# Seven products instead of plain units for the keys of the first 1024 tokens in the third layer

## The chip, the cores and the metric

The kernel runs on one core of one Trainium2 chip. The metric is the device time of one launch in microseconds (us). Before the change, three runs took 1438.44, 1438.20 and 1438.22 us, median 1438.22. The profiled execution, from which every row below comes, took 1439.99 us.

A core has engines that run side by side, each with its own instruction queue which it works off strictly in order: TensorE (PE; PEld are its weight loads), VectorE (DVE), ScalarE (ACT), GpSimd (POOL), and SyncE (SP), which here only issues DMAs. Semaphores make an instruction wait for one on another engine or for a DMA; everything behind it on its own engine then waits as well.

## The reference, cut to what matters

```
def _A_ref(x, wqkv, wo):                 # x: 2048 tokens x 1024, 32 heads of 32
    q, k, v = heads of (x @ wqkv)
    phi = lambda t: jnp.where(t > 0, t + 1, jnp.exp(t)) + 1e-6
    pq, pk = phi(q), phi(k)
    kv = einsum("bhsd,bhse->bhde", pk, v)
    z = sum of pk over the tokens
    ...
x = x + _A_ref(_layernorm(x), A_wqkv, A_wo)
x = x + _B_ref(_layernorm(x), B_W_gate, B_W_up, B_W_down)
x = x + _A_ref(_layernorm(x), A_wqkv, A_wo)      # the third layer, l = 2 in the code
x = x + _B_ref(_layernorm(x), B_W_gate, B_W_up, B_W_down)
```

`_B_ref` is a feed-forward block (1024 to 3584 and back). Everything comes in bf16. What counts below is one thing: in the third layer the queries and keys are products of normalised rows and the columns of `wqkv`, and `phi` is applied to every element of both.

## The kernel before

**Tiles.** The 2048 tokens are four quarters of 512, each of QT = 4 row tiles of 128 tokens. The normalised rows of a quarter are turned by transposing DMAs (L423) into `xnT` tiles, which are the stationary operand of the matmuls. Column halves of 512 of a weight matrix (`k0`, `k1`, `q0`, `q1`) are the moving operand. A plain unit is one row tile times one column half: eight matmuls of 128x512 into one PSUM bank (`project`, L506), followed by `phi`: a relu on ACT out of PSUM (L448), an exponential on ACT (L449), and a join on DVE (L452). For keys, POOL then adds the rows up (`k_sum`, L525 for the first, L527 for the others).

**Seven products.** `blocks(p, first)` computes the same for two quarters at once with a scheme of Strassen's kind: the input is cut into halves of tokens (the two quarters) and of the inner dimension, the weight into halves of the inner dimension and of columns, and seven products replace eight. Each product is four matmuls (`mm`, L690). It needs four sums of the inputs (`sums_x`, L1272 to L1275, on DVE, 16 instructions for two quarters) and four sums of the weight, which an earlier layer left in DRAM and which two DMAs of 1 MB bring in (`tq0`, `tq1` for the queries, `tk0`, `tk1` for the keys; L472). For row tile j the seven products go through four accumulators, qx, qy, qv, qz, in four steps: `one` does mm1 into qx, copies it to qy (L681 on DVE or L683 on ACT), does mm5 into qv and copies that to `qm`; `two` does mm2 into qx (which is then finished and gets its `phi`), mm6 into qy and qz = qy + qm on DVE (L712); `three` does mm7 into qy, qm = qy + qm on DVE (L716) with its `phi`, and mm3 into qz with its `phi`; `four` does mm4 into qy with its `phi`. So mm2 waits for the copy of qx, mm7 for the sum qz, and mm4 for the sum qm.

**The third layer before.** First the keys of quarter 0 by plain units (eight of them), then the queries of quarters 0 and 1 by seven products, with the plain units of the keys of quarter 1 between the steps, two to each j; then the queries of quarter 2 by plain units, then the keys of quarters 2 and 3 by seven products.

**What sets the order.** The emitting Python code calls the steps and units one after another, and each call is followed by a tick. Side work is due at a number of ticks (`later.at`): layer normalisation of the rows of quarters 2 and 3 (statistics, then the scaling of one row tile on DVE, `ln_scale` L183, at the ticks of the table LN_AT, which isn't changed), sums, sends of x to DRAM (`away`, L283), and early sums of quarter 3 for a later stage (the functions `n1`, `n2`, `n3`, `k1`, all of them `op`, L559, four instructions for each row tile, by `make_early`).

**Where tiles lie.** `slot` takes all large tiles of 8 KB per partition, the weights included, from one pool of 16. A tile that gets the place of an older one may be written only when the last reader of the older one is done; which place it gets follows from the order of requests. The scaled rows of quarter 3 are four L183 into one such tile, here called slab2_2. In the kernel before it has the place of the last weight tile of the layer before, which is read for the last time before the third layer begins.

**Weights.** The `ring` loads weights by SP in the order of a plan (`plan_A`), each as soon as its place is free (L40, L472).

Of the kernel before, what the change touches and what calls it, by code (L numbers as in the profile page):

```python
# [14 lines left out]
P = 128  # L15
# [77 lines left out]
class _Net:  # L93
# [372 lines left out]
    def plan_A(self, l):  # L466
        D = self.D
        cols = {"k0": D, "k1": D + NW, "v0": 2 * D, "v1": 2 * D + NW, "q0": 0, "q1": NW}
        for n in ("k0", "k1", "v0", "q0", "q1", "v1", "o0", "o1") if l == 0 else (
                "k0", "k1", "q0", "q1", "tq0", "tq1", "tk0", "tk1", "v0", "v1", "o0", "o1"):  # L470
            if n[0] == "t":
                self.ring.add((l, n), lambda t, n=n: self.nc.sync.dma_start(  # L472
                    out=t[:, :, :].bitcast(F16), in_=self.tw[n[1:]]))
# [6 lines left out]
    def layer_A(self, l, last_ln):  # L480
# [14 lines left out]
        turns = count()  # L495
        by_row = lambda a: a.rearrange("p (i b d) -> p i b d", i=R, d=HD)

        def project(name, l_q, j, between=None):
            w = ring.get((l, name))

            spare = l_q < self.NQ - 1 and next(turns) % 3 == 2 and not (l and l_q < 2)
# [19 lines left out]
        def k_sum(t, cols):  # L521

            pk = self.pk_home(l, t)[:, cols]
            if t == 0:
                nc.gpsimd.tensor_copy(out=ksum[:, cols], in_=pk)  # L525
            else:
                nc.gpsimd.tensor_tensor(out=ksum[:, cols], in0=ksum[:, cols], in1=pk, op=ALU.add)  # L527
# [128 lines left out]
        def blocks(p, first):  # L656
# [4 lines left out]
            r0, r1, t0, t1 = (ring.get((l, n)) for n in (f"{p}0", f"{p}1", f"t{p}0", f"t{p}1"))  # L661
# [23 lines left out]
            def steps(j):  # L685
# [7 lines left out]

                def one():
                    S["X"] = self.ps.tile([P, NW], F32, tag="a", name=f"qx{j}")
                    mm(1, S["X"], True)
                    if p == "k" and j == 2:
# [3 lines left out]
                    copy(S["Y"], S["X"], p == "k" and j)  # L701
                    v = self.kvp.tile([P, NW], F32, tag=f"kv{j % 2 if p == 'q' or j < 2 else 0}", name=f"qv{j}")
                    mm(5, v, True)
                    S["V"] = self.temp(name="qm5")
                    copy(S["V"], v, p == "k" and j)

                def two():
                    mm(2, S["X"])
                    put(S["X"], 0, j, 0)
# [183 lines left out]
        else:  # L893
            ring.load_to(ring.index((l, "tq1")) + 1)
            for j in range(QT):
                later.at(1 + j, lambda j=j: self.sums_x(l, 0, j))
# [7 lines left out]
        else:  # L904
            first = column_major(k_unit, 0)
# [10 lines left out]
        else:  # L916
            run(first)
            k = iter(row_major(k_unit, 1))
            Q = blocks("q", 0)
            todo = [Q[0][0]]  # L920
            for j in range(QT):
                todo += [next(k), Q[j][1], next(k), Q[j][2]] + ([Q[j + 1][0]] if j + 1 < QT else []) + [Q[j][3]]
            q2 = row_major(q_unit, 2)
            make_early([(16 + 3 * j, QT + j) for j in range(QT)], n1, n2, n3, k1)
            run(todo[:-1] + q2[:1] + todo[-1:])
            later.at(1, lambda: ring.load_to(ring.index((l, "tk1")) + 1))
            self.xs[l, 1] = [self.x[self.NS + i][:, :].bitcast(F16).rearrange("p (a n) -> p a n", n=NW)
                             for i in range(QT)]
            for j in range(QT):
                later.at(4 + j, lambda j=j: self.sums_x(l, 1, j))  # L930
            run(q2[1:])
            K = blocks("k", 2)
# [879 lines left out]
```

## Time and profile before

| what | from the profile before |
|---|---|
| median of three runs | 1438.22 us |
| profiled execution | 1439.99 us, of which 1437.9 us are the span of the instructions |
| PE busy | 1427.1 us (99%) |
| DVE, ACT, POOL busy | 1045.2, 623.3, 309.3 us |
| third layer, keys and queries | 730.4 to 821.6 us: PE busy 90.56 of 91.27 us |
| granted clock of PE | full in all 40 slices |

A line of the table of groups reads: line, engine, operation, out<-in, shape, count | busy us, mean ns. A line of a timeline reads: start, duration, engine, line, operation, count, and in brackets the idle time ahead of it with what ended it. Neighbouring instructions of one kind are merged (x4), and the end of an instruction overlaps the start of the next, so that the price of one among its like is the distance between starts.

### The profile page before, as it was taken

To read this page: it belongs to the slowest core of one execution; us is meant where nothing else is said; L and a number is where in the kernel's file an instruction comes from. 1 tells how busy PE (TensorE), PEld (TensorE's weight loads), DVE (VectorE), ACT (ScalarE), POOL (GpSimd) and SP (SyncE) were. 2 spreads that over 40 slices of the span, in tenths; PEclk is the share of its full clock that TensorE was granted. 3 is DMA by queue.
4 is the path that set the end of the run, shared out by engine and by line. 5 is a ranking of instruction groups with operands and counts; after the bars stand their busy time and mean duration, and the time that the engine had idled before them with its cause. 6 is when DMAs were issued, how large, how long until landed. Compare 5 with 4: busy or idle time off the path is not lost.

```text
span 1437.9 us, 21394 instructions
## 1 busy us (share of the span) xinstructions
PE 1427.1 (99%) x7720; PEld 739.7 (51%) x7748; DVE 1045.2 (73%) x2013; ACT 623.3 (43%) x1143; POOL 309.3 (22%) x220
## 2 busy tenths in 40 slices
PE   9999999999999999999999999999999999999998
PEld 4444444444455444545654444445554565555557
DVE  7978698778685666558778886866766864766895
ACT  7872564333325244332058725733443433444301
POOL 1453860010100011110032477510111011111102
PEclk9999999999999999999999999999999999999999
DMA  9950787898559999966983218998878699975575
GB/s 286 240 162 8 172 209 202 278 335 288 200 192 294 323 367 345 291 216 199 302 277 93 70 22 234 287 274 262 268 225 294 228 304 335 274 229 174 193 260 183
DMA packets 367865, 337.74 MB, mean 235 GB/s; under 512 B 110032, under 2 KB 327760, under 8 KB 366736
## 3 DMA queue, kind: packets, MB, share of 16 engines
q1 hardware_dynamic: 359184, 313.57, 73.1%
q10 hardware_dynamic: 7136, 18.88, 3.4%
q0 software_dynamic: 1440, 3.93, 0.7%
q8 instruction: 60, 0.98, 0.3%
q14 instruction: 45, 0.37, 0.1%
HBM read 246.87 MB, written 64.82 MB: 217 GB/s over the span
## 4 chain that ended last, share of the span: by engine, by line
PE 91%; DVE 3%; DMA 2%; ACT 2%; SPq 1%; issue 1%; ACTq 0%; DVEq 0%
PE ps L506 11%; PE yu L1301 9%; PE yg L1301 9%; PE xg L1301 6%; PE xu L1301 6%; PE dy L1447 6%; PE dx L1447 5%; PE i L1154 5%; PE ps L789 4%; PE zu L1301 3%; PE zg L1301 3%; PE my L588 3%; PE dyT L1489 2%; PE mv L588 2%; PE mx L588 2%; PE dy L1489 2%
## 5 line engine op out<-in xcount | busy, mean ns | idle before, releaser
L1301 PEld LDWEIGHTS <-w 128*128 128x128 f16 (+1 forms) x2768 | 270.4, 98 | 297.2 <-issue 4.6
L506 PE MATMUL ps<-w,xnT 128*128 128x512 bf16 x768 | 169.9, 380 | 0.6 <-ACT xnT L361 0.2
L1381 POOL TENSOR_TENSOR h<-m5u,m5g 128x512 f16<-128x512 f32 x28 | 37.1, 1326 | 425.3 <-DVE m5u L1377 252.5
L506 PEld LDWEIGHTS <-xnT 128*128 128x128 bf16 x768 | 74.4, 98 | 90.3 <-issue 1.8
L1301 PE MATMUL xg<-xnT,w 128*128 128x512 f16 x448 | 115.5, 379 | 0.0
L1301 PE MATMUL xu<-xnT,w 128*128 128x512 f16 x448 | 115.0, 380 | 0.0
L1489 PEld LDWEIGHTS <-h 128*128 128x128 f16 x1008 | 98.6, 98 | 12.9
L1381 POOL TENSOR_TENSOR h<-c22u,c22g 128x512 f16<-128x512 f32 x28 | 36.0, 1285 | 289.8 <-DVE c22u L1377 247.8
L1447 PEld LDWEIGHTS <-h 128*128 128x128 f16 x616 | 60.3, 98 | 71.8 <-issue 0.3
L1301 PE MATMUL yu<-s,w 128*128 128x512 f16 x376 | 96.5, 379 | 0.5 <-DVE zu L1357 0.5
L1301 PE MATMUL yg<-s,w 128*128 128x512 f16 x376 | 96.9, 379 | 0.0
L449 ACT ACTIVATE e<-e,eps 128x512 f32<-128x512 f32 x128 | 91.0, 720 | 3.2
L736 POOL TENSOR_TENSOR kvc<-pq,kvc 128x1024 f32<-128x1024 bf16 x32 | 78.5, 2452 | 53.1 <-DVE den L741 32.8
L789 PE MATMUL ps<-T,pqT 128*128 128x512 bf16 x374 | 83.0, 380 | 0.5
L1328 DVE TENSOR_TENSOR h<-yu,r 128x512 f16<-128x512 f32 x56 | 38.6, 690 | 53.8 <-PE yu L1301 53.8
L1325 ACT ACTIVATE r<-yg 128x512 f32<-128x512 f32 x56 | 33.4, 597 | 101.3 <-PE yg L1301 101.3
L527 POOL TENSOR_TENSOR kvc<-kvc,slab 128x512 f32<-128x512 f32 x46 | 57.2, 1249 | 75.9 <-DVE slab L452 72.7
L1447 PE MATMUL dx<-w,h 128*128 128x512 bf16 x327 | 72.5, 380 | 0.5
L448 ACT ACTIVATE e<-ps 128x512 f32<-128x512 f32 x92 | 54.2, 590 | 28.4 <-PE ps L506 27.9
L1154 PEld LDWEIGHTS <-x 128*128 128x128 f16 x504 | 49.3, 98 | 33.5 <-issue 1.9
L1325 ACT ACTIVATE r<-zg 128x512 f32<-128x512 f32 x56 | 32.9, 587 | 76.7 <-PE zg L1301 76.7
L748 POOL TENSOR_TENSOR pq<-pq,den 128x1024 bf16<-128x1024 bf16 x32 | 61.1, 1909 | 6.8 <-DVE den L743 6.8
(286 smaller groups left out, 2630.6 us busy)
## 6 DMA issues: line engine op xcount, KB each, us to landing
w<-in_B_W_gate_dram SPq DMA_DIRECT2D x56, 512.0 KB, 6.4
w<-in_B_W_up_dram SPq DMA_DIRECT2D x56, 512.0 KB, 6.0
w<-ddT SPq DMA_DIRECT2D x21, 896.0 KB, 6.4
w<-td SPq DMA_DIRECT2D x18, 896.0 KB, 5.0
w<-dd SPq DMA_DIRECT2D x18, 896.0 KB, 5.9
x<-away SPq DMA_DIRECT2D x30, 512.0 KB, 7.5
away<-x SPq DMA_DIRECT2D x24, 512.0 KB, 8.1
w<-in_B_W_down_dram SPq DMA_DIRECT2D x12, 896.0 KB, 6.1
```

Of the source, the lines that this page charges most:

```text
L449: self.last_exp = nc.scalar.activation(out=e, in_=e, func=ACT.Exp, scale=-1.0, bias=self.eps6[:, 0:1])
L506: nc.tensor.matmul(by_row(ps), lhsT=self.xnT[l, l_q][:, kt, j * P:(j + 1) * P], rhs=w[:, kt, :].rearrange("p (b i d) -> p i b d", i=R, d=H ...
L588: nc.tensor.matmul(banks[j], lhsT=A(i)[:, j * P:(j + 1) * P], rhs=B(i), start=start and i == 0, stop=i == NS - 1, skip_group_check=True)
L736: nc.gpsimd.tensor_tensor(out=prod, in0=pq_of[sc, j], in1=zrow, op=ALU.mult)
L748: nc.gpsimd.tensor_tensor(out=heads(pq), in0=heads(pq), in1=den[:, :].unsqueeze(2).to_broadcast([P, D // HD, HD]), op=ALU.mult)
L789: nc.tensor.matmul(ps, lhsT=pqT[sc][:, g, j * P:(j + 1) * P], rhs=T[g // 4][:, g % 4, n2 * NW:(n2 + 1) * NW], start=(g == 0), stop=(g == G ...
L1154: nc.tensor.matmul(b[:, w, :], lhsT=B[p][:, w, k, :], rhs=A[p][:, k, :], start=start and w == 0 and k == 0, stop=k == 1, skip_group_check= ...
L1301: nc.tensor.matmul(ps, lhsT=W[w][m][:, k, :], rhs=A[m][:, k, :], start=start and k == 0, stop=k == 3, skip_group_check=True)
L1325: self.last_relu = nc.scalar.activation(out=out, in_=ps, func=ACT.Relu)
L1381: nc.gpsimd.tensor_tensor(out=h[:, 3, :], in0=V["u"], in1=V["g"], op=ALU.mult)
L1447: nc.tensor.matmul(banks[j], lhsT=A(k)[:, j * P:(j + 1) * P], rhs=w[:, i, :], start=start and k == 0, stop=k == self.U - 1, skip_group_che ...
L1489: nc.tensor.matmul(out, lhsT=A[i // 2][:, i % 2, j * P:(j + 1) * P], rhs=B[m][:, i, :], start=start and i == 0 and j == 0, stop=i == NK - ...
```

## The change

The keys of quarters 0 and 1 of the third layer are computed by `blocks("k", 0)`, in the interleaving that the keys of quarters 2 and 3 had already (row tiles 0 and 1 in turns, then 2 and 3). For that:

- The plan of weights loads `tk0` and `tk1` right behind `k0`, and loads them a second time (`tk0b`, `tk1b`) for the late keys: two more DMAs of 1 MB.
- The sums of quarters 0 and 1 (16 DVE instructions, L1275 to L1278 after the change) move from the first ticks of the layer into the end of the down phase of the layer before.
- Between the steps of the queries there is one plain unit to each j instead of two, and it is one of the queries of quarter 2, so that fewer of these are left for the stretch behind.
- For keys `one` is mm1, copy and then mm2 (`second`), and mm5 with its copy (`fifth`) stands at the head of `two`. The early keys' copies all go to ACT; the late ones keep the split of before.
- The early sums of quarter 3 are due at ticks 8 + 3j of the queries' run instead of 16 + 3j, the sums of quarters 2 and 3 at 1 + j of the last plain units; plain units of this layer use only one of the two kinds of PSUM banks.

The core of the diff:

```diff
--- before.py
+++ after.py
@@ -467,10 +467,10 @@
         D = self.D
         cols = {"k0": D, "k1": D + NW, "v0": 2 * D, "v1": 2 * D + NW, "q0": 0, "q1": NW}
         for n in ("k0", "k1", "v0", "q0", "q1", "v1", "o0", "o1") if l == 0 else (
-                "k0", "k1", "q0", "q1", "tq0", "tq1", "tk0", "tk1", "v0", "v1", "o0", "o1"):
+                "k0", "tk0", "tk1", "k1", "q0", "q1", "tq0", "tq1", "tk0b", "tk1b", "v0", "v1", "o0", "o1"):
             if n[0] == "t":
                 self.ring.add((l, n), lambda t, n=n: self.nc.sync.dma_start(
-                    out=t[:, :, :].bitcast(F16), in_=self.tw[n[1:]]))
+                    out=t[:, :, :].bitcast(F16), in_=self.tw[n[1:3]]))
             elif n[0] == "o":
                 c = NW * int(n[1])
                 self.ring.add((l, n), self.wo_v[:, :, c:c + NW])
@@ -492,13 +492,13 @@
 
 
         R = P // HD
-        turns = count()
+        turns, summed = count(), set()
         by_row = lambda a: a.rearrange("p (i b d) -> p i b d", i=R, d=HD)
 
         def project(name, l_q, j, between=None):
             w = ring.get((l, name))
 
-            spare = l_q < self.NQ - 1 and next(turns) % 3 == 2 and not (l and l_q < 2)
+            spare = not l and l_q < self.NQ - 1 and next(turns) % 3 == 2
             ps = (self.ps3 if spare else self.ps).tile([P, NW], F32, tag="b" if spare else "a")
             for kt in range(KT):
                 if between and kt == KT - 2:
@@ -521,7 +521,8 @@
         def k_sum(t, cols):
 
             pk = self.pk_home(l, t)[:, cols]
-            if t == 0:
+            if cols.start not in summed:
+                summed.add(cols.start)
                 nc.gpsimd.tensor_copy(out=ksum[:, cols], in_=pk)
             else:
                 nc.gpsimd.tensor_tensor(out=ksum[:, cols], in0=ksum[:, cols], in1=pk, op=ALU.add)
@@ -658,7 +659,8 @@
 
             xa, xb = self.xnT[l, first], self.xnT[l, first + 1]
             s1, s2, s3, s4 = self.xs[l, first // 2]
-            r0, r1, t0, t1 = (ring.get((l, n)) for n in (f"{p}0", f"{p}1", f"t{p}0", f"t{p}1"))
+            late = "b" if (p, first) == ("k", 2) else ""
+            r0, r1, t0, t1 = (ring.get((l, n)) for n in (f"{p}0", f"{p}1", f"t{p}0{late}", f"t{p}1{late}"))
             t0, t1 = (t[:, :, :].bitcast(F16) for t in (t0, t1))
             A = {1: xa[:, 0:4], 2: xa[:, 4:8], 3: s4, 4: xb[:, 4:8], 5: s1, 6: s2, 7: s3}
             B = {1: r0[:, 0:4], 2: r0[:, 4:8], 3: r1[:, 4:8], 4: t1[:, 0:4], 5: t0[:, 0:4],
@@ -691,22 +693,28 @@
                                          rhs=B[m][:, k, :].rearrange("p (b i d) -> p i b d", i=R, d=HD),
                                          start=start and k == 0, stop=k == 3, skip_group_check=True)
 
+                def fifth():
+                    v = self.kvp.tile([P, NW], F32, tag=f"kv{0 if late and j > 1 else j % 2}", name=f"qv{j}")
+                    mm(5, v, True)
+                    S["V"] = self.temp(name="qm5")
+                    copy(S["V"], v, late and j)
+
+                def second():
+                    mm(2, S["X"])
+                    put(S["X"], 0, j, 0)
+
                 def one():
                     S["X"] = self.ps.tile([P, NW], F32, tag="a", name=f"qx{j}")
                     mm(1, S["X"], True)
-                    if p == "k" and j == 2:
+                    if late and j == 2:
                         S["Y"] = self.kvp.tile([P, NW], F32, tag="kv1", name=f"qy{j}")
                     else:
                         S["Y"] = self.ps3.tile([P, NW], F32, tag="b", name=f"qy{j}")
-                    copy(S["Y"], S["X"], p == "k" and j)
-                    v = self.kvp.tile([P, NW], F32, tag=f"kv{j % 2 if p == 'q' or j < 2 else 0}", name=f"qv{j}")
-                    mm(5, v, True)
-                    S["V"] = self.temp(name="qm5")
-                    copy(S["V"], v, p == "k" and j)
+                    copy(S["Y"], S["X"], late and j)
+                    (second if p == "k" else fifth)()
 
                 def two():
-                    mm(2, S["X"])
-                    put(S["X"], 0, j, 0)
+                    (fifth if p == "k" else second)()
                     mm(6, S["Y"])
                     S["Z"] = self.ps.tile([P, NW], F32, tag="a", name=f"qz{j}")
                     nc.vector.tensor_tensor(out=S["Z"], in0=S["Y"], in1=S["V"], op=ALU.add)
@@ -892,8 +900,6 @@
             steps = self.head()
         else:
             ring.load_to(ring.index((l, "tq1")) + 1)
-            for j in range(QT):
-                later.at(1 + j, lambda j=j: self.sums_x(l, 0, j))
         for i in range(QT if l == 0 else self.NS, self.ST):
             at, lag = (8 + 3 * (i - QT), 2) if l == 0 else LN_AT[i - self.NS]
             self.ln_at(at, l, i, lag)
@@ -901,8 +907,6 @@
                 later.at(at + 3, lambda i=i: self.send_away(i))
         if l == 0:
             first = self.head_units(lambda *a: k_unit(0, *a), lambda *a: q_unit(0, *a), *steps)
-        else:
-            first = column_major(k_unit, 0)
 
         def quarter0():
             self.phi_lag = 3 if l == 0 else 0
@@ -914,23 +918,22 @@
                                                   mybir.EngineType.Activation}):
                 quarter0()
         else:
-            run(first)
-            k = iter(row_major(k_unit, 1))
+            in_turns = lambda b: [b[j + i][n] for j in (0, 2) for n in range(4) for i in range(2)]
+            run(in_turns(blocks("k", 0)))
             Q = blocks("q", 0)
+            q2 = row_major(q_unit, 2)
             todo = [Q[0][0]]
             for j in range(QT):
-                todo += [next(k), Q[j][1], next(k), Q[j][2]] + ([Q[j + 1][0]] if j + 1 < QT else []) + [Q[j][3]]
-            q2 = row_major(q_unit, 2)
-            make_early([(16 + 3 * j, QT + j) for j in range(QT)], n1, n2, n3, k1)
-            run(todo[:-1] + q2[:1] + todo[-1:])
-            later.at(1, lambda: ring.load_to(ring.index((l, "tk1")) + 1))
+                todo += [Q[j][1], q2[j], Q[j][2]] + ([Q[j + 1][0]] if j + 1 < QT else []) + [Q[j][3]]
+            make_early([(8 + 3 * j, QT + j) for j in range(QT)], n1, n2, n3, k1)
+            run(todo)
+            ring.load_to(ring.index((l, "tk1b")) + 1)
             self.xs[l, 1] = [self.x[self.NS + i][:, :].bitcast(F16).rearrange("p (a n) -> p a n", n=NW)
                              for i in range(QT)]
             for j in range(QT):
-                later.at(4 + j, lambda j=j: self.sums_x(l, 1, j))
-            run(q2[1:])
-            K = blocks("k", 2)
-            run([K[j + i][n] for j in (0, 2) for n in range(4) for i in range(2)])
+                later.at(1 + j, lambda j=j: self.sums_x(l, 1, j))
+            run(q2[QT:])
+            run(in_turns(blocks("k", 2)))
         for q in range(1, self.NQ - 1) if l == 0 else ():
             if (l, q) == (0, 1):
                 for i in range(self.U // 2 - 2):
@@ -1511,7 +1514,7 @@
             entry(1)
             mm(6, S2, y)
             for o, i, b in zip(halves(z), ys, halves(m5)):
-                v.tensor_tensor(out=o, in0=i, in1=b, op=ALU.add)
+                self.last_dz = v.tensor_tensor(out=o, in0=i, in1=b, op=ALU.add)
             later.tick()
             mm(2, a12, x)
             put(0, 0, x, True)
@@ -1747,7 +1750,10 @@
                 self.ln_chunk(l, 1, 20, 3, 3, after)
             elif not final:
                 self.ln_later(l + 1, 0, 24, 3, 4, held)
-                self.ln_later(l + 1, 1, 36, 3, 4, held)
+                self.ln_later(l + 1, 1, 35, 3, 4, held)
+                for j in range(QT):
+                    self.later.at((46, 47, 49, 51)[j], lambda j=j: self.behind(
+                        self.last_on if j < 2 else self.last_dz, lambda j: self.sums_x(l + 1, 0, j), (j,)))
             for n in range(2 if (l, c) in ((1, 1), (3, 0)) else 0):
                 self.later.at(2 + n, lambda t=n + (c == 0) * self.NS: self.bring_back(t))
             self.down(l, c, hT, final)
```

Beside the numbers of lines (L690 becomes L692, L712 becomes L720, L716 L724, L559 L560, L683 L685, L1272 to L1275 become L1275 to L1278), three places of the order matter below.

First DVE around the queries' last row tile, before. qz_7279 and qm_7232 belong to row tile 2, qz_7388 to row tile 3, slab_2_7245 is the tile of quarter 3's scaled rows, and pq are the finished queries.

```order
1011 L183 TENSOR_SCALAR slab_2_7245<-x,mv,rstd 128x1024
1012 L716 TENSOR_TENSOR qm_7232<-qy_7225,qm_7232 128x512
1013 L452 SCALAR_TENSOR_TENSOR x<-ps,e 128x512
1014 L559 TENSOR_TENSOR x<-x,slab_2_7245 128x512
1015 L559 TENSOR_TENSOR x<-x 128x512 x3
1016 L452 SCALAR_TENSOR_TENSOR pq_1_7035<-qm_7232,e 128x512
1017 L452 SCALAR_TENSOR_TENSOR pq_0_7034<-qz_7279,e 128x512
1018 L183 TENSOR_SCALAR slab_2_7245<-x,mv,rstd 128x1024
1019 L452 SCALAR_TENSOR_TENSOR pq_1_7035<-qy_7225,e 128x512
1020 L559 TENSOR_TENSOR x<-x,slab_2_7245 128x512
1021 L559 TENSOR_TENSOR x<-x 128x512 x3
```

The same place after the change. qz_7378 is row tile 2, qz_7459 row tile 3, slab_2_7262 the tile of the scaled rows.

```order
1023 L452 SCALAR_TENSOR_TENSOR pq_0_7176<-qz_7378,e 128x512
1024 L183 TENSOR_SCALAR slab_2_7262<-x,mv,rstd 128x1024 x2
1025 L560 TENSOR_TENSOR x<-x,slab_2_7262 128x512
1026 L560 TENSOR_TENSOR x<-x 128x512 x3
1027 L560 TENSOR_TENSOR x<-x,slab_2_7262 128x512
1028 L560 TENSOR_TENSOR x<-x 128x512 x3
1029 L183 TENSOR_SCALAR slab_2_7262<-x,mv,rstd 128x1024 x2
1030 L560 TENSOR_TENSOR x<-x,slab_2_7262 128x512
1031 L560 TENSOR_TENSOR x<-x 128x512 x3
1032 L452 SCALAR_TENSOR_TENSOR pq_1_7177<-qy_7341,e 128x512
1033 L452 SCALAR_TENSOR_TENSOR pq_0_7176<-qx_7424,e 128x512
1034 L720 TENSOR_TENSOR qz_7459<-qy_7429,qm_7436 128x512
```

What were four L183 apart, with joins and sums of the products between, is now one run: four L183 and twelve L560 stand between the joins of row tile 2 and the sum qz of row tile 3. The tile of the scaled rows has another place too: it takes that of the `xnT` tile of quarter 0, whose last reader is mm2 of row tile 3 of the queries, so the first L183 of this run waits for that product on PE.

Behind that sum, on DVE still, the sum qm of row tile 3 follows after four L560 and nine of the sums of quarters 2 and 3:

```order
1036 L560 TENSOR_TENSOR x<-x 128x512 x3
1037 L1275 TENSOR_TENSOR x<-xnT_3_7465 128x4x128
1038 L1277 TENSOR_TENSOR x<-xnT_2_7025,xnT_3_7465 128x4x128
1039 L1276 TENSOR_TENSOR x<-x,xnT_2_7025 128x4x128
1040 L1275 TENSOR_TENSOR x<-xnT_3_7465 128x4x128
1041 L1278 TENSOR_TENSOR x<-xnT_2_7025,x 128x4x128
1042 L1276 TENSOR_TENSOR x<-x,xnT_2_7025 128x4x128
1043 L1277 TENSOR_TENSOR x<-xnT_2_7025,xnT_3_7465 128x4x128
1044 L1278 TENSOR_TENSOR x<-xnT_2_7025,x 128x4x128
1045 L1275 TENSOR_TENSOR x<-xnT_3_7465 128x4x128
1046 L724 TENSOR_TENSOR qm_7436<-qy_7429,qm_7436 128x512
```

In the kernel before, nothing but one L183 stood between the two (qz_7388, then qm_7338). On PE, the twelve matmuls between mm2 of row tile 3 and its mm7 (mm6 and one plain unit) and the ten between mm7 and mm4 (mm7, mm3 and two of a plain unit) are what runs meanwhile.

Last ACT where the early keys end and the queries begin, after the change. qm_7079, qz_7085 and qy_7045 are row tile 2 of the keys, qm_7098, qz_7104 and qy_7062 row tile 3; qv_7185 and qx_7178 are row tile 0 of the queries.

```order
608 L448 ACTIVATE e<-qm_7079 128x512
609 L448 ACTIVATE e<-qz_7085 128x512
610 L449 ACTIVATE e<-e,eps_137 128x512 x2
611 L448 ACTIVATE e<-qm_7098 128x512
612 L448 ACTIVATE e<-qz_7104 128x512
613 L449 ACTIVATE e<-e,eps_137 128x512 x2
614 L448 ACTIVATE e<-qy_7045 128x512
615 L448 ACTIVATE e<-qy_7062 128x512
616 L449 ACTIVATE e<-e,eps_137 128x512 x2
617 L176 ACTIVATE rstd<-mv,eps_139 128x1
618 L685 ACTIVATE qm_7190<-qv_7185 128x512
```

The copies of the first query products (row 618 and the one of qx_7178 right behind it) stand behind three groups of two relus and two exponentials. Before the change there was no such place: the queries began behind plain units, whose `phi` is one relu and one exponential at a time. Further on, for each j of the queries, the order on ACT stays as it was: relu of qm, relu of qz, two exponentials, copy of the next qx; on PE the stretch between mm7 of one row tile and mm2 of the next was mm7, mm3, mm1, mm4 and a plain unit, and is now the same without the plain unit.

## The prediction

> **What bounds the kernel now.** I read the page's shares first, then the table of stretches for the third layer's keys and queries, then the chain of waits, then the timelines of PE, ACT and DVE.
>
> ```profile
> span 1437.9 us, 21394 instructions
> PE 1427.1 (99%) x7720; PEld 739.7 (51%) x7748; DVE 1045.2 (73%) x2013; ACT 623.3 (43%) x1143; POOL 309.3 (22%) x220
> PEclk9999999999999999999999999999999999999999
> ```
>
> PE has 10.8 us without a matmul in the whole span (1437.9 - 1427.1). So a matmul saved is worth its full time, and a stall of PE made anew costs its full time; both count alike.
>
> ```profile
> 720.00:730.37 10.37, 10.37 (x96) 9.23 (x95) 5.22 (x9) 1.18 (x2) 0.00 (x0) 1.00 1.02 356
> 730.37:821.64 91.27, 90.56 (x419) 40.77 (x417) 77.98 (x141) 72.11 (x133) 32.17 (x27) 1.00 0.42 125
> 744.00:786.00 42.00, 41.82 (x194) 18.89 (x193) 33.65 (x54) 35.43 (x71) 13.00 (x11) 1.00 0.27 58
> ```
>
> The columns are the length, then busy time of PE, PEld, DVE, ACT and POOL, then PE's clock, the DMA share and GB/s. In the layer's stretch (second row) PE is busy 90.56 of 91.27 us, but DVE is busy 77.98 (85%) and ACT 72.11 (79%). Neither has much to give. During the queries (third row) PE idles 0.18 us. The question is thus whether ACT and DVE keep up when PE has less to do and their work stands otherwise.
>
> **The saving.** Keys of 1024 tokens are 16 plain units of 8 matmuls, 128; seven products make 112 of them. Sixteen matmuls go, their weight loads with them.
>
> ```profile
> 730.37 13.81 PE ps L506 x64
> ```
>
> This row of the chain gives 13.81 / 64 = 0.216 us for one. Saved: 16 x 0.216 = 3.45 us. The other work changes little in amount: as many relus, exponentials and joins; four more copies for ACT and as many more pairs of sums qz and qm for DVE.
>
> **ACT between mm7 and the next mm2.** Before, the queries go as follows on PE, then on ACT:
>
> ```profile
> 751.36 1.03 PE L690 MATMUL qy<-w,s 128*128 128x512 f16 x4
> 752.22 1.03 PE L690 MATMUL qz<-w,s 128*128 128x512 bf16 x4
> 753.09 1.03 PE L690 MATMUL qx<-w,xnT 128*128 128x512 bf16 x4
> 753.95 0.60 PE L690 MATMUL qv<-w,s 128*128 128x512 f16 x2
> 754.38 1.03 PE L690 MATMUL qy<-w,xnT 128*128 128x512 f16 x4
> 755.24 1.89 PE L506 MATMUL ps<-w,xnT 128*128 128x512 bf16 x8
> 756.97 1.03 PE L690 MATMUL qx<-w,xnT 128*128 128x512 bf16 x4
> ```
>
> ```profile
> 753.24 0.61 ACT L448 ACTIVATE e<-qm 128x512 f32<-128x512 f32 x1
> 753.76 0.58 ACT L448 ACTIVATE e<-qz 128x512 f32<-128x512 f32 x1
> 754.23 1.32 ACT L449 ACTIVATE e<-e,eps 128x512 f32<-128x512 f32 x2
> 755.46 0.58 ACT L683 ACTIVATE qy<-qx 128x512 f32<-128x512 f32 x1
> 758.93 0.28 ACT L176 ACTIVATE rstd<-mv,eps 128x1 f32<-128x1 f32 x1
> 759.12 0.57 ACT L448 ACTIVATE e<-qx 128x512 f32<-128x512 f32 x1
> ```
>
> mm7 starts at 751.36. The relu of qm starts 1.88 us later, the group of two relus and two exponentials takes 2.22 (753.24 to 755.46), the copy of qx 0.58: it ends 4.68 us after mm7's start, at 756.04. The next mm2, at 756.97, doesn't notice, because a plain unit of 1.73 us lies between. After the change that unit is gone from there. PE has mm7, mm3, mm1, mm4 = 16 matmuls, 3.45 us, and then waits for the copy. For row tile 0 the small L176 stands ahead of the copy too (0.19 between the last two rows): 4.87 - 3.45 = 1.42. For row tile 1 three matmuls of a split mm5 help: 4.68 - 19 x 0.216 = 0.58. Row tile 2: 4.68 - 3.45 = 1.23. Together **3.2 us**. The bound below is nothing, if the groups were to start earlier than in the row; it can't be far from 3.2, since mm7 itself (1.03) and the sum qm on DVE come first.
>
> **The seam between keys and queries.** From mm7 of key row tile 2 on, ACT has three such groups (order above, rows 608 to 616), L176 and the copy of the first qv; mm5 of query row tile 2 needs that bank of PSUM back. ACT: 1.88 + 3 x 2.22 + 0.19 + 0.58 = 9.31. PE has until there 34 matmuls, 7.34. Stall **2.0 us**. Inside the keys the same happens once, more mildly: qy of row tile 2 takes the bank of row tile 0's qy, whose join must be done. ACT: 1.88 + 2 x 2.22 + relus and the first exponential 1.71 (two starts 0.52 and 0.47 apart, and 0.72), the join 0.69, the copy 0.58 = 9.30, against 40 matmuls, 8.63: 0.67. I add 0.24 for mm7 of row tile 2, which waits for qz behind a join. Together **0.9 us**; between nothing and twice that.
>
> **DVE at the queries' last row tile.** This is the largest term. These are DVE's rows at the same place before:
>
> ```profile
> 770.49 1.32 DVE L183 TENSOR_SCALAR slab<-x,mv,rstd 128x1024 bf16<-128x1024 f32 x1
> 772.93 0.41 DVE L559 TENSOR_TENSOR x<-x,slab 128x512 f16<-128x512 bf16 x1
> 773.26 2.05 DVE L559 TENSOR_TENSOR x<-x 128x512 f16<-128x512 bf16 x3
> 775.23 0.68 DVE L452 SCALAR_TENSOR_TENSOR pq<-qm,e 128x512 bf16<-128x512 f32 x1
> 776.57 0.81 DVE L183 TENSOR_SCALAR slab<-x,mv,rstd 128x1024 bf16<-128x1024 f32 x1
> 777.29 0.69 DVE L452 SCALAR_TENSOR_TENSOR pq<-qy,e 128x512 bf16<-128x512 f32 x1
> 777.89 0.42 DVE L559 TENSOR_TENSOR x<-x,slab 128x512 f16<-128x512 bf16 x1
> 778.23 1.09 DVE L559 TENSOR_TENSOR x<-x 128x512 f16<-128x512 bf16 x3
> 779.23 0.69 DVE L452 SCALAR_TENSOR_TENSOR x<-ps,e 128x512 bf16<-128x512 f32 x1
> 779.83 0.69 DVE L452 SCALAR_TENSOR_TENSOR pq<-qx,e 128x512 bf16<-128x512 f32 x1
> 780.43 0.69 DVE L712 TENSOR_TENSOR qz<-qy,qm 128x512 f32<-128x512 f32 x1
> 792.20 0.42 DVE L1272 TENSOR_TENSOR x<-xnT 128x512 f16<-128x512 bf16 x1
> 792.53 0.42 DVE L1274 TENSOR_TENSOR x<-xnT,xnT 128x512 f16<-128x512 bf16 x1
> ```
>
> By distances of starts, an L183 is 0.72, four L559 1.34, a join 0.60, a sum qz or qm about 0.69, one of the L1272 kind 0.33. Before, this work is spread out, and a sum that PE needs is never more than a few instructions away. After the change four L183, twelve L560 and two joins stand ahead of qz of row tile 3, and none of it can start before mm2 of that row tile is done, since the scaled rows take the place of the `xnT` tile that mm2 reads last. From that moment DVE needs 4 x 0.72 + 3 x 1.34 + 2 x 0.60 + 0.69 = 8.8 us, and PE has 12 matmuls, 2.59. mm7 waits **6.2 us**. Then qm: four L560 (1.34), nine sums (3.0) and qm (0.68) make 5.0 us, against ten matmuls, 2.16. mm4 waits **2.9 us**. The last sums wait for transposing DMAs of the new rows; those have the 8.8 us to land.
>
> The bounds: a POOL instruction beside them makes these dearer. L183 took 1.32 at 770.49, and four L559 took 2.30 from 772.93 to 775.23, with this one on POOL:
>
> ```profile
> 773.15 1.21 POOL L527 TENSOR_TENSOR kvc<-kvc,x 128x512 f32<-128x512 f32 x1 [1.89 <-DVE x L452]
> ```
>
> At those prices the two waits would grow by 4 x 0.60 + 4 x 0.96 = 6.2. I take the cheap ends: L527 adds up keys, and no keys are made near this place any more. The cheap ends are also the floor.
>
> **What I cost at nothing.** That plain units use one kind of banks only: four of them are there, and no two plain units follow each other closely among the queries any more. The 16 sums of quarters 0 and 1 go into 720 to 730, where DVE is busy 5.22 of 10.37 us (first of the three rows of stretches); at 0.33 each they need 5.4, so they just fit. If not, the last adds of that phase are late by a few tenths: 0 to 0.3. The weights: `tk0` and `tk1` are issued where one query half and `tq0` were:
>
> ```profile
> 723.54 0.53 SPq L40 DMA_DIRECT2D w<-in_A_wqkv_dram  x1
> 724.18 4.36 SPq L472 DMA_DIRECT2D w<-tq  x2
> ```
>
> ```profile
> w<-in_A_wqkv_dram SPq DMA_DIRECT2D x1, 1024.0 KB, 11.2
> w<-tq SPq DMA_DIRECT2D x1, 1024.0 KB, 13.1
> ```
>
> They took 11.2 and 13.1 us to land, at 734.7 and 737.3. mm5 needs `tk0` at 16 matmuls after 730.3, at 733.7, and mm6 `tk1` at 734.6. With these latencies PE would wait 2.7 us. I take nothing, as the two MB of `k0` and `k1` that were ahead of them in the queues until 723 to 724 aren't there now; 0 to 2.7 goes into the range. The second loads of `tk0` and `tk1` are issued during the waits of the last row tile and have over 10 us until the late keys. The late keys hardly change.
>
> **The sum.** -3.45 + 3.2 + 2.0 + 0.9 + 6.2 + 2.9, less the 0.18 that the queries wait already (their third row of stretches), is +11.6 us. On the profiled execution that is 1439.99 + 11.6 = 1451.6. The median of the runs lies 1.77 below the profiled one: 1438.22 + 11.6 = **1449.8 us**.
>
> **The rivals.** What a measurement of this kernel tells from no change is 0.2%, 2.9 us: 1435.3 to 1441.1 counts as the same.
>
> First, that ACT and DVE keep ahead. If side work got out of the way at the last row tile, and ACT's groups came earlier, only the saving would be left: 1438.2 - 3.45 = 1434.8. For it speaks that PE waits only 0.71 us in the whole stretch before; against it, the copy's 4.68 us in the rows and 85% of DVE. Faster; chance 0.05.
>
> Second, that only the run on DVE is milder than counted: the first L183 doesn't wait for mm2, and DVE does it a row tile earlier in its idle time. Then ACT's stalls stay: -3.45 + 3.2 + 2.0 + 0.9 - 0.18 = +2.5, 1440.7, the same by the bound. Against it speaks the place of the tile; it would need the order of places to be another at run time. With half of the run absorbed it is 1445. Chance 0.07 for the first, 0.10 for the half.
>
> Third, the weights are late: +2.7, 1452.5. For it, the latencies above; against it, the emptier queue. Chance 0.10.
>
> Fourth, PE's clock. This is the longest wait of PE before, by the table of waits (engine, line, what ended it, us in total, times, longest):
>
> ```profile
> PE idle L302 <- DVE e L299: 1.4, 1, 1.4
> ```
>
> Nothing is longer, and the clock is full in every slice, so no row here shows what a wait of 6.2 us does to it. If it halves, each matmul until it is back costs 0.216 us more. The ten behind the long wait would then take 4.3 us, and DVE's 5.0 up to qm hide that. What runs slowly behind the wait for qm is not hidden: 1.7 us for eight matmuls, 3.5 for sixteen. I take eight, since the products between the waits count towards the recovery: 1451.5. The Trainium skill states such a rule ("TensorE: Matmul & The Clock Gate", HAM oscillation): a gap of more than about 3.4 us re-throttles PE to half rate, and about as long a busy time is needed to come back. By that rule only the wait for qz is long enough, and the 2.9 us for qm isn't. Chance 0.25.
>
> My own case as counted: 0.43. Faster 0.05, same 0.07, slower 0.88. The likeliest case alone lies between 1446 and 1453 (without the milder terms of ACT, about 3; with half of POOL's contention, 3). The range is 1443.5 to 1455.
>
> **What would show it.** PE's waits after should have mm7 of a query behind the sum L720 for about 6 us and mm4 behind L724 for about 3 within 10 us, with four L183 and twelve L560 on DVE in between; copies L685 on ACT as the end of waits of 1 to 2 us ahead of mm2, and the longest at the seam; no wait on a DMA at the layer's start; PE busy 3.4 us less in all. It is wrong if DVE has scaled quarter 3's rows before mm2 of row tile 3 is over, if PE's waits in the queries stay under a few us, or if the time is below 1441.

## The result

The changed kernel takes 1451.07 us (median of four runs, 1450.77 to 1452.47) against 1438.33 for the kernel before in the same job: 12.7 us or 0.9% slower, ratio 1.009 with a 95% interval of 1.0073 to 1.0108. Forecast were 1449.8 us and a range of 1443.5 to 1455. The profiled execution took 1451.36 us, 11.4 more than the one of before, and its span is 1449.6 us, 11.7 more.

The page's shares after the change:

```profile
span 1449.6 us, 21384 instructions
PE 1426.4 (98%) x7704; PEld 738.4 (51%) x7732; DVE 1049.4 (72%) x2021; ACT 625.7 (43%) x1151; POOL 309.4 (21%) x220
```

The sixteen matmuls are gone (7720 to 7704), but PE is busy only 0.7 us less, where the prediction's signs had 3.4: matmuls at half speed count as busy longer, and those between 794.83 and 799.78 below account for about 2 us of the difference. PE is without a matmul for 23.2 us instead of 10.8. The table of PE's waits (engine, line, what ended it, us in total, times, longest) names them:

```profile
PE qy L692 <- DVE qz L720: 6.3, 1, 6.3
PE qx L692 <- ACT qy L685: 3.3, 4, 1.2
PE qv L692 <- ACT qm L685: 1.8, 1, 1.8
...
PE qy L692 <- DVE qm L724: 1.0, 1, 1.0
PE qx L692 <- DVE qy L683: 0.9, 1, 0.9
```

All of these lie in the third layer, and none of them ends with a DMA. PE's timeline shows the places; a wait is in brackets:

```profile
756.01 1.46 PE L692 MATMUL qv<-w,s 128*128 128x512 f16 x6
759.23 0.81 PE L692 MATMUL qv<-w,s 128*128 128x512 f16 x3 [1.76 <-ACT qm L685]
...
766.13 1.03 PE L692 MATMUL qy<-w,xnT 128*128 128x512 f16 x4
768.39 1.02 PE L692 MATMUL qx<-w,xnT 128*128 128x512 bf16 x4 [1.23 <-ACT qy L685]
...
786.62 1.89 PE L506 MATMUL ps<-w,xnT 128*128 128x512 bf16 x8
794.83 1.86 PE L692 MATMUL qy<-w,s 128*128 128x512 f16 x4 [6.32 <-DVE qz L720]
796.49 1.91 PE L692 MATMUL qz<-w,s 128*128 128x512 bf16 x4
798.19 0.63 PE L506 MATMUL ps<-w,xnT 128*128 128x512 bf16 x1
799.78 1.02 PE L692 MATMUL qy<-w,xnT 128*128 128x512 f16 x4 [0.95 <-DVE qm L724]
800.64 6.85 PE L506 MATMUL ps<-w,xnT 128*128 128x512 bf16 x31
```

The wait in brackets counts from the modelled end of the matmul ahead; what it costs is read from start to start. From 786.62, eight matmuls at 0.216 end at 788.35, and mm7 starts at 794.83: 6.48 us. The same way mm4 costs 799.78 - 794.83 - 10 x 0.216 = 2.79, the seam 1.92, the three copies inside the queries 1.40, 0.55 and 1.29, and the two places inside the early keys 1.03 together.

On DVE the run stands as the order had it:

```profile
785.96 1.53 DVE L183 TENSOR_SCALAR slab<-x,mv,rstd 128x1024 bf16<-128x1024 f32 x2 [0.88 <-PE qx L692]
...
790.09 1.53 DVE L183 TENSOR_SCALAR slab<-x,mv,rstd 128x1024 bf16<-128x1024 f32 x2
...
794.08 0.69 DVE L720 TENSOR_TENSOR qz<-qy,qm 128x512 f32<-128x512 f32 x1
...
799.03 0.69 DVE L724 TENSOR_TENSOR qm<-qy,qm 128x512 f32<-128x512 f32 x1
```

It waits for PE's qx, which is mm2 of row tile 3, starts at 785.96 and has qz ready at 794.77, 8.8 us later. Where the layer's keys and queries begin and end on PE, first before (the row of L588 is the first matmul behind them), then after (the row of qy is their last):

```profile
730.21 5.13 PE L506 MATMUL ps<-w,xnT 128*128 128x512 bf16 x23
...
821.21 0.38 PE L588 MATMUL mx<-x,xn 128*128 128x512 bf16 x1
```

```profile
729.51 3.62 PE L692 MATMUL qx<-w,xnT 128*128 128x512 bf16 x16
...
831.77 1.24 PE L692 MATMUL qy<-w,xnT 128*128 128x512 f16 x5
```

Five matmuls at 0.216 from 831.77 end at 832.85. The stretch grew from 91.00 to 103.34 us, by 12.34. The waits above are 15.46; less the saving of 3.45 and the 0.18 of before they make 11.83, and 0.5 more is in the late keys, which took 25.52 us (from 807.33) instead of 25.05 (from 796.16).

### The profile page after: what moved, and what is told of

The parts are those of the page before. It is cut to its first block, busy times and chain, and to the rows that moved or that the text cites. A ratio compares the mean times of both kernels' runs of the same rounds, so it can differ in the third digit from the quotient of the medians.

```text
span 1449.6 us, 21384 instructions
## 1 busy us (share of the span) xinstructions
PE 1426.4 (98%) x7704; PEld 738.4 (51%) x7732; DVE 1049.4 (72%) x2021; ACT 625.7 (43%) x1151; POOL 309.4 (21%) x220
## 4 chain that ended last, share of the span: by engine, by line
PE 90%; DVE 5%; ACT 2%; DMA 1%; issue 1%; SPq 0%; DVEq 0%
PE ps L506 9%; PE yu L1304 9%; PE yg L1304 9%; PE dy L1450 7%; PE xg L1304 6%; PE xu L1304 6%; PE i L1157 5%; PE dx L1450 5%; PE ps L797 4%; PE zu L1304 3%; PE zg L1304 3%; PE my L589 3%; PE dy L1492 2%; PE mv L589 2%; PE mx L589 2%; PE dyT L1492 2%
## 5 line engine op out<-in xcount | busy, mean ns | idle before, releaser
L506 PE MATMUL ps<-w,xnT 128*128 128x512 bf16 x640 | 141.7, 380 | 0.3 <-ACT xnT L361 0.2
L506 PEld LDWEIGHTS <-xnT 128*128 128x128 bf16 x640 | 61.8, 98 | 75.2 <-issue 1.6
L1450 PE MATMUL dy<-w,h 128*128 128x512 f16 x280 | 61.4, 379 | 0.0
```

Of the source, the lines that this page charges most:

```text
L506: nc.tensor.matmul(by_row(ps), lhsT=self.xnT[l, l_q][:, kt, j * P:(j + 1) * P], rhs=w[:, kt, :].rearrange("p (b i d) -> p i b d", i=R, d=H ...
L1450: nc.tensor.matmul(banks[j], lhsT=A(k)[:, j * P:(j + 1) * P], rhs=w[:, i, :], start=start and k == 0, stop=k == self.U - 1, skip_group_che ...
```

## The experiments

Every ratio is against the kernel before, run in the same job. The edits are to the changed kernel unless said otherwise.

### e1: another place for the scaled rows

```diff
-                "k0", "tk0", "tk1", "k1", "q0", "q1", "tq0", "tq1", "tk0b", "tk1b", "v0", "v1", "o0", "o1"):
+                "k0", "tk0", "tk1", "k1", "q0", "q1", "tq0", "tq1", "tk0b", "tk1b", "k1b", "v0", "v1", "o0", "o1"):
...
-            r0, r1, t0, t1 = (ring.get((l, n)) for n in (f"{p}0", f"{p}1", f"t{p}0{late}", f"t{p}1{late}"))
+            r0, r1, t0, t1 = (ring.get((l, n)) for n in (f"{p}0", f"{p}1{late}", f"t{p}0{late}", f"t{p}1{late}"))
```

> The change with one thing more: the key weights k1 are loaded a second time for the late keys, so that their place of 8 KB is free meanwhile, and the scaled rows of quarter 3 get it instead of the place of quarter 0's turned rows. In the order on DVE the four L183 and the L560 then stand apart again. Theory (place): the first L183 waits for mm2 of row tile 3 only because of the place; the waits for qz (6.3 us) and qm (0.95) of row tile 3 and PE's slow matmuls behind them (about 1.9) go, the waits for ACT's copies stay (about 5 in all): 1451.1 - 9.1 = 1442.0 us, between 1440.5 and 1443.5, PE's clock full. Rival (load): DVE and ACT are simply too full in this layer, and a run taken away there comes back as other waits for DVE: above 1446.

Measured: 1442.55 us, ratio 1.003 (1.0018 to 1.0041). The place was the cause of the run: the first L183 now starts 15 us before mm2 of row tile 3 (785.73), and the four stand apart, between 770.19 and 784.73. With one tile more to be had, 8.5 us of the 12.7 are gone; the wait for qz of row tile 3 fell from 6.3 to 0.86, PE's clock stayed full, and the copies' waits stayed:

```profile
770.19 0.81 DVE L183 TENSOR_SCALAR slab<-x,mv,rstd 128x1024 bf16<-128x1024 f32 x1
```

```profile
PE qx L692 <- ACT qy L685: 2.2, 3, 1.2
PE qv L692 <- ACT qm L685: 1.8, 1, 1.8
...
PE qy L692 <- DVE qz L720: 0.9, 1, 0.9
```

So DVE being full isn't the main cause: the same instructions, spread out, cost PE 2 us (0.9 at the sums qz, 1.0 at the sums qm).

### e2 and e3: two plain units to each j, with and without the free place

```diff
-                todo += [Q[j][1], q2[j], Q[j][2]] + ...
+                todo += [q2[2 * j], Q[j][1], q2[2 * j + 1], Q[j][2]] + ...
...
-            run(q2[QT:])
+            run(q2[2 * QT:] + [lambda: None])
```

e2 has this and the edit of e1; e3 has this alone.

> As the one before (k1 loaded again), and two plain units of quarter 2's queries to each j of the queries, one ahead of mm2 and one ahead of mm7, so that no plain unit is left between the queries and the late keys. Theory (cover): the waits of mm2 for ACT's copies inside the queries (1.2, 0.4, 1.1) and most of the one at the seam (1.8) go, since a plain unit of 1.73 us lies between: 1442.0 - 4.3 = 1437.7, between 1436 and 1440. Rival: the late keys begin 7 us earlier for ACT and DVE, and their input sums or copies are late instead: 1440 or more, with new waits at the late keys.

> The change with two plain units to each j, but without the second load of k1: the scaled rows of quarter 3 keep the place of quarter 0's turned rows, and the run of L183 and L560 on DVE stays in one piece ahead of qz of row tile 3. Theory (cover and place, each with its own price): the copies' waits go (-4.3), the wait for qz stays at 6 to 6.5 us, the one for qm grows, since more sums stand ahead of it and fewer matmuls beside it (2 to 3.7): 1446 to 1450. If cover alone were the cause, this comes out near 1438.

Measured: e2 1444.50 us, ratio 1.0042 (1.0028 to 1.0056), as the rival had it, though the largest new wait is one for a weight, which it didn't name; e3 1448.70, ratio 1.0072 (1.0057 to 1.0087), within the theory's range, though not by its terms. In both, the waits for copies inside the queries and at the seam are gone. In e2, PE's timeline and stretches show what replaced them (stretches: bounds, length, busy time of PE, PEld, DVE, ACT, POOL, PE's clock, DMA share, GB/s):

```profile
794.29 1.67 PE L692 MATMUL qx<-w,xnT 128*128 128x512 bf16 x7
799.20 1.01 PE L692 MATMUL qv<-w,x 128*128 128x512 f16 x2 [3.23 <-DMA w<-tk]
800.00 1.91 PE L692 MATMUL qx<-w,xnT 128*128 128x512 bf16 x4
```

```profile
799.00:803.00 4.00, 3.80 (x12) 1.47 (x12) 0.06 (x1) 1.01 (x2) 0.00 (x0) 0.63 1.02 381
```

The second load of tk0 stands on SP behind the four transposing DMAs of the new rows (L423, 788.01 to 793.37); it is issued at 793.80 and lands 5.4 us later. The place of tq0 isn't what holds it: mm7 of row tile 3, the last to read tq0, is over at 791.4. With no plain units behind the queries the late keys stand and wait for it, 3.23 us, and then run at a clock of 0.63. The plain units at the end were cover for that load. In e3 the wait for qz is 7.8 us, not 6 to 6.5: the run on DVE stays in one piece, and four L560 more (1.34 us) stand in it. Behind it the matmuls stay slow for longer than in the changed kernel (see the clock, below). The waits for copies go without the second load of k1 (e3), and the wait for qz goes with that load alone (e1): cover for ACT and the place are two separate prices.

### e4: matmuls in the long wait

```diff
                 def three():
+                    if p == "q" and j == 3:
+                        fill = self.kvp.tile([P, NW], F32, tag="kv0", name="fill")
+                        for k in range(24):
+                            nc.tensor.matmul(fill, lhsT=xb[:, k % 8, 0:P], rhs=r0[:, k % 8, :],
+                                             start=k == 0, stop=k == 23, skip_group_check=True)
                     mm(7, S["Y"])
```

> The change with 24 matmuls more, of 128x512 into a bank that nobody reads, put on PE right ahead of mm7 of row tile 3 of the queries (5.2 us of PE in the middle of the wait of 6.3 us). Theory (clock hidden): the clock stays full, the wait left for qz is about 1.1 us, the one for qm goes from 0.95 back to 2.9, and the time is that of the change, 1451.1 within 0.7. Rival (clock costs its own): without the half clock about 1.9 us come back, 1449.2.

Measured: 1448.77 us, ratio 1.0072 (1.0057 to 1.0087), 2.3 us less than the change, though PE does 24 matmuls more. By the time alone the rival would have it, but the rows say otherwise. The matmuls also changed the order on DVE: three sums of quarters 2 and 3 stand ahead of qm now, where the change has nine. Six of the 24 ran ahead of mm2 of row tile 3, so that 2.43 us of the wait for qz are left instead of 1.1.

```profile
785.14 1.53 DVE L183 TENSOR_SCALAR slab<-x,mv,rstd 128x1024 bf16<-128x1024 f32 x2 [0.88 <-PE qx L692]
...
793.25 0.70 DVE L720 TENSOR_TENSOR qz<-qy,qm 128x512 f32<-128x512 f32 x1
...
796.19 0.70 DVE L729 TENSOR_TENSOR qm<-qy,qm 128x512 f32<-128x512 f32 x1
```

```profile
789.69 1.89 PE L506 MATMUL ps<-w,xnT 128*128 128x512 bf16 x8
794.01 1.02 PE L692 MATMUL qy<-w,s 128*128 128x512 f16 x4 [2.43 <-DVE qz L720]
...
796.94 1.02 PE L692 MATMUL qy<-w,xnT 128*128 128x512 f16 x4 [0.83 <-DVE qm L729]
```

From the first L183 to qm it is 11.05 us here and 13.07 in the changed kernel (799.03 - 785.96). The difference of 2.02 is six sums of 0.335. In both kernels mm4 starts 0.75 us after qm does, at full clock here (four matmuls in 1.02) and behind ten slow ones there. So the slow clock cost the changed kernel nothing at that place, because DVE ended the stretch; 2.0 of the 2.3 us are the six sums. The run wasn't a clean test of the clock alone.

### e5 and e6: moving what is left

e5 is e1 with a plain unit ahead of mm2 of row tiles 0 and 1 and two instead of four behind the queries; e6 is e5 with the early sums (L560) due ten ticks later.

```diff
-                todo += [Q[j][1], q2[j], Q[j][2]] + ...
+                a, b = ((1, 1), (1, 1), (0, 1), (0, 1))[j]
+                todo += [next(u) for _ in range(a)] + [Q[j][1]] + [next(u) for _ in range(b)] + [Q[j][2]]
...
-            make_early([(8 + 3 * j, QT + j) for j in range(QT)], n1, n2, n3, k1)
+            make_early([(18 + 3 * j, QT + j) for j in range(QT)], n1, n2, n3, k1)
```

> The run e1 (k1 loaded a second time) with two of the four plain units that were left behind the queries put elsewhere: one ahead of mm2 of the queries' row tile 0 (the seam), one ahead of mm2 of row tile 1. Theory (cover, each place with its own price): the waits there, 1.76 and 1.23 us in the profile of e1, go: 1442.55 - 3.0 = 1439.6, between 1438.8 and 1440.6. Rival (as in the run with two units everywhere): with two plain units behind the queries instead of four the second loads of tk are late, and the late keys wait for them: above 1441.

> The run above with the L560 of quarter 3 due ten ticks later, so that they stand behind the queries' last sums on DVE. Theory: the last waits of mm7 and mm4 for DVE within the queries (0.25, 0.86 and 0.76 in the profile of e1) go: 1 to 1.8 us less than the run above, near 1438. Rival: the L560 then stand ahead of the late keys' copies on DVE, and mm2 and mm7 of the late keys wait as much: no gain, or a loss up to 2.

Measured: e5 1441.25 us, ratio 1.002 (1.001 to 1.0029); e6 1444.03, ratio 1.0038 (1.0023 to 1.0052). In e5 the seam's wait and the one of row tile 1 went, as foreseen, but only 1.3 of the 3.0 us came through; PE now waits for DVE and the copy at row tiles 2 and 3. The time lies where the rival put it, above 1441, but its reason isn't there: no wait in the layer ends with a DMA. These are the waits:

```profile
PE qy L692 <- DVE qz L720: 1.6, 2, 1.0
PE qx L692 <- ACT qy L685: 1.2, 2, 0.7
PE qy L692 <- DVE qm L724: 1.1, 2, 0.7
```

In e6 the L560 reach the late keys, and the longest wait is there, mm2 behind a copy on DVE. The rival's mechanism held, and the loss of 2.8 us is more than the 2 that it allowed:

```profile
817.25 1.02 PE L692 MATMUL qx<-w,xnT 128*128 128x512 bf16 x4 [2.19 <-DVE qy L683]
```

### e7: the sums of quarters 0 and 1 at the layer's start again

This is e1 without the sums in the down phase; `sums_x(l, 0, j)` is called for all four j right at the start of the layer.

> The run e1 with the 16 sums of quarters 0 and 1 on DVE at the start of the layer again, instead of in the down phase ahead. Theory (as the prediction had it, the move hides them): at the start they are late for mm5 and mm7 of the early keys; 16 x 0.33 = 5.4 us on DVE against 3.45 us of PE before mm5 of row tile 0, and the first ones are enough for it: 0.5 to 2.5 us slower than e1, 1443 to 1445. Rival: only the first eight are needed early, and PE doesn't notice: 1442.5 within 0.5.

Measured: 1450.85 us, ratio 1.0084 (1.0069 to 1.0099), 8.3 us slower than e1, more than expected. PE waits at mm5 for the first sum, and again, 17 us later, for a copy, each time with slow matmuls soon behind:

```profile
729.26 3.62 PE L692 MATMUL qx<-w,xnT 128*128 128x512 bf16 x16
735.75 1.04 PE L692 MATMUL qv<-w,s 128*128 128x512 f16 x4 [2.88 <-DVE s L1277]
...
752.63 2.49 PE L692 MATMUL qx<-w,xnT 128*128 128x512 bf16 x8 [2.52 <-ACT qy L685]
```

On DVE the first sum stands behind the statistics of the rows that the phase before finished last and behind two joins, which the expectation had not counted:

```profile
730.44 3.06 DVE L166 BATCH_NORM_STATS2 stats<-x 128x6 f32<-128x512 f32 x5
733.43 0.69 DVE L452 SCALAR_TENSOR_TENSOR x<-qx,e 128x512 bf16<-128x512 f32 x1
...
735.28 0.41 DVE L1277 TENSOR_TENSOR s<-xnT 128x512 f16<-128x512 bf16 x1
```

Moving the sums ahead is thus the part of the change that early keys by seven products can't do without, and it was hidden: the changed kernel's PE has no wait there.

### b1: the cover removed in the kernel before

```diff
             k = iter(row_major(k_unit, 1))
+            run([next(k) for _ in range(QT)])
...
-                todo += [next(k), Q[j][1], next(k), Q[j][2]] + ...
+                todo += [Q[j][1], next(k), Q[j][2]] + ...
```

The early sums are due four ticks earlier, so that they keep their places.

> The kernel before with one part of the change alone: one plain unit to each j of the queries instead of two, the one ahead of mm2 left out; the four plain units of keys that are over run ahead of the queries, so that nothing else is added or saved. The early sums of quarter 3 stand at the same places. Theory (cover): mm2 of row tiles 1, 2 and 3 waits for ACT's copy as in the changed kernel, 1.4, 0.55 and 1.3 us from start to start: 1438.4 + 3.2 = 1441.6, between 1440.6 and 1442.6, with PE's waits on copies L683 in the table. Rival: without the change's other work ACT has time to spare there and copies earlier: 1438.4 within 0.7.

Measured: 1445.04 us, ratio 1.0049 (1.0032 to 1.0065): dearer than the theory, and not for its reason. Row tiles 1 and 2 lost 0.3 and 0.6 us to the copy; the largest wait is a plain unit's, for a bank of PSUM that the join of finished queries on DVE has to give back, and the eleven matmuls behind it took 4.00 us to the next start (785.10) instead of 2.4:

```profile
781.10 4.16 PE L506 MATMUL ps<-w,xnT 128*128 128x512 bf16 x11 [3.01 <-DVE pq L452]
```

```profile
781.00:785.00 4.00, 3.90 (x11) 1.43 (x11) 1.96 (x4) 0.03 (x1) 0.00 (x0) 0.57 0.26 50
```

So taking away the unit ahead of mm2 costs the kernel before 6.5 us too, but how the price splits up depends on what stands around it: matmuls of a later mm5 filled part of the gap here. The four units moved ahead of the queries are part of this edit, so it isn't the cover alone.

### e9: the early sums on POOL

This is e5 with the sixteen L560 issued to POOL instead of DVE.

> The run e5 (k1 loaded a second time, units at the seam) with the 16 early sums of quarter 3 (L560) on POOL instead of DVE. POOL is idle there. Theory (DVE too full at the queries' end): the waits of mm7 and mm4 of row tiles 2 and 3 for DVE and of mm2 of row tile 3 for its copy, 0.56, 0.99, 0.44, 0.69 and 0.67 in e5's profile, go: 1441.25 - 3.0 = 1438.3, between 1437.3 and 1439.3, level with the kernel before. Rival (shared access): with POOL busy beside it DVE's L183 and L1275 take 1.3 us instead of 0.8 and 0.4, as L183 and L559 did beside L527 in the profile before: no gain, 1440.5 or more.

Measured: 1440.50 us, ratio 1.0015 (1.0006 to 1.0025), the lowest of all variants, 0.75 us less than e5 (the intervals of the two ratios overlap) and still slower than before. The theory's range is missed, and the time is at the rival's bound: the waits for qz are gone, but L183 on DVE takes 1.2 to 1.55 us beside POOL, and mm2 waits for ACT's copies and mm4 behind sums that wait for a transposing DMA:

```profile
771.14 1.55 DVE L183 TENSOR_SCALAR slab<-x,mv,rstd 128x1024 bf16<-128x1024 f32 x1
```

```profile
PE qx L701 <- ACT qy L694: 2.7, 3, 1.2
PE qy L701 <- DVE qm L733: 1.6, 1, 1.6
```

No variant beat the kernel before.

## Why the prediction was right

**The run on DVE (6.2 and 2.9 us).** Measured 6.48 and 2.79 from start to start. The prices by distances of starts held to 0.1 us (8.8 us from the first L183 to qz); the 0.3 on top is mostly the 0.2 from the end of mm2, where mm6 starts (785.76), to the first L183 (785.96). As to POOL, the cheap ends were right since it had nothing to do, and e1 shows the cause: with another place for the scaled rows 8.5 us come back.

**ACT inside the queries (3.2 us).** Measured 1.40 + 0.55 + 1.29 = 3.24 against 1.42 + 0.58 + 1.23. The chain mm7, sum, relus, exponentials, copy of 4.68 us in the profile before carried over: for row tile 0, with L176 in it, it took 4.80 us (763.54 to 768.34) against 4.87. In e2 and e3 a plain unit ahead of mm2 takes these waits away. b1 limits what may be concluded: the same unit taken out of the kernel before cost more, by another wait.

**The seam and the early keys (2.0 and 0.9 us).** Measured 1.92 and 1.03. e5 removed the seam's wait with one plain unit there.

**The saving (3.45 us).** PE has sixteen matmuls fewer; it was used up elsewhere. Of copies on ACT there are eight more, not four (1143 to 1151 instructions), two for each row tile; the sum has no term for their number.

**What was costed at nothing.** The sums in the down phase cost PE nothing: no wait of PE stands between 700 us and the layer, though DVE is busy 9.44 of the last 9.51 us ahead of it. e7 shows that at the layer's start they would have cost 8.3 us. No plain unit of the layer waits for a bank. The weights came in time. The two early tk took 6.5 us to land (the median, by the table of DMA issues), not 11.2 and 13.1, and no wait in the layer ends with a DMA:

```profile
w<-tk SPq DMA_DIRECT2D x2, 1024.0 KB, 6.5
```

"The late keys hardly change" was too low by 0.5 us: their mm2 waits 0.86 us for a copy on DVE, and this is most of what the sum of 11.6 lacks to the 12.34 of the layer. The profiled times differ by only 11.4, mostly since the layer began 0.7 us earlier in the profile after. Over the variants it began between 728.4 and 731.2 us. In b1, whose program is that of before up to this layer, it began at 728.52 instead of 730.21, so the spread isn't all due to the change; it was not looked into.

**The clock.** The rival's mechanism was there; its price was not, in this profile. PE's stretches in the changed kernel:

```profile
794.80:798.20 3.40, 3.37 (x9) 1.14 (x9) 3.40 (x11) 0.00 (x0) 0.00 (x0) 0.50 0.17 25
...
799.80:803.00 3.20, 3.20 (x15) 1.44 (x15) 3.20 (x8) 3.20 (x7) 0.00 (x0) 1.00 1.01 369
```

Behind the wait of 6.3 us the clock was 0.50, and the ten matmuls between qz and qm ran at half speed; the wait for qm shrank to 0.95 for it, as worked out. But from mm4 on the clock was full again, so the 1.7 us that the rival put behind it didn't come.

That this term stayed away is in part luck. In e3 the same comes in the same order, the wait for qz, ten matmuls at half speed and a wait of 0.95 us for qm, but mm4 and what follows it are still slow:

```profile
803.00 1.86 PE L692 MATMUL qy<-w,xnT 128*128 128x512 f16 x4 [0.95 <-DVE qm L724]
804.66 3.70 PE L692 MATMUL qx<-w,xnT 128*128 128x512 bf16 x11
808.21 1.46 PE L692 MATMUL qv<-w,x 128*128 128x512 f16 x6
```

Fifteen matmuls take 5.21 us there instead of 3.24, so 2.0 us aren't hidden, about what the rival had. The four executions of the changed kernel point the same way: a mean clock of 0.998 goes with spans of 1449.0 us (twice), 0.997 with 1449.6 and 0.996 with 1450.7. Only the one of 1449.6 has a trace, so where the longest lost its time isn't shown.

## What to carry to other kernels

A change that saves matmuls on an engine that is 99% busy is judged by what the other engines must finish between one product and the next: write down, for each product that waits, the chain on ACT or DVE from the last product it needs, in distances of starts from the profile, and hold it against the matmuls that lie between. One tile more in a full pool can cost more than the work saved, since it decides which old tile's last reader a new writer waits for, and on an engine that works in order this holds up everything behind. Plain work between dependent products is cover; moving it to one gap opens another, and here no arrangement tried paid for sixteen matmuls.

## What the runs showed of the hardware

How short a wait slows PE's clock was not expected. Behind a wait of 2.43 us (e4) four matmuls took 1.02 us, full speed; behind waits of 2.52 (e7), 3.01 (b1), 3.23 (e2), 6.32 (the change) and 7.76 us (e3) the clock was between 0.50 and 0.68 over the next three to five us, though in e7 and e2 not all of the matmuls right behind the wait were slow. The Trainium skill ("TensorE: Matmul & The Clock Gate", HAM oscillation) puts the gap at more than about 3.4 us; in these runs shorter ones were enough. Where the limit lies one trace of each doesn't say. A wait on an engine that runs at the limit can so cost half as much again as its length: the 3.01 us in b1 brought 1.6 us of slow matmuls with it, while the 6.32 us of the changed kernel brought none in its profile, because DVE set the pace there.
